# Block-selected attention and a gated network: a new recorded order of the five queues

## The chip, the cores and the metric

One core of a Trainium2 chip. The metric is the device time of one execution in microseconds (us). The kernel before took 310.41, 308.06 and 309.83 us in three runs, median 309.83.

In the profile PE is TensorE (PEld its weight loads), DVE is VectorE, ACT is ScalarE, POOL is GpSimd, SP is SyncE, which only issues transfers. L949 is line 949 of the kernel before.

## What is computed

Attention over 4 batches, 8 heads, 768 positions and 64 channels, in which each query sees only the 6 chunks of 32 keys with the highest upper bounds; then, on the 3072 tokens of 512 channels that come out, an RMS norm and a gated network of width 1536.

```python
k_min, k_max = k_chunks.min(axis=3), k_chunks.max(axis=3)
ub = sum(maximum(q * k_min, q * k_max), axis=-1)      # upper bound of each chunk
top_chunks = argsort(where(causal, ub, -1e9))[..., -6:]
scores = where(selected & (pos_q >= pos_k), scale * q @ k.T, -1e9)
attn_out = softmax(scores) @ v
xn = x / sqrt(mean(x * x) + 1e-6) * rms_g              # x: attn_out, heads side by side
g = xn @ w_gate
out = ((g * sigmoid(g)) * (xn @ w_val)) @ w_out
```

## The kernel before

The work is cut into twelve blocks of 256 tokens, (batch, third of the sequence), in the order of the list `ORDER`: (0,0), (1,0), (2,0), (3,0), (0,1), (1,1), (0,2), (2,1), (1,2), (3,1), (2,2), (3,2). "Block 0" below is (0,0). A block has an attention part for each of two groups of four heads, a norm, and a network part.

**Attention part.** SP (at the start ACT too) loads `kraw`, `qraw`, `vraw`. VectorE transposes them into `kT`, `qT` (`turn k`, `turn q`, L621) and takes the minimum and maximum of each chunk (`ext`, L636). `half k` and `half q` (L628, L629) convert to bf16 on ScalarE or GpSimd. TensorE forms the upper bounds (`upper`, L507 or L525), VectorE turns them round (`ubn`, L550), finds the sixth largest (`top`, L566), compares (`mk`, L572) and turns the mask back (`mt`, `swap`). TensorE forms the scores (L749) with the mask added by matmul (L760), ScalarE the exponential (L799), GpSimd zeroes the triangle (`tri`, L769), TensorE multiplies by the values (`values`, L825), VectorE divides (`rden` L840, `norm` L844). From the second third on, a copy of the queries (`qx`, L677) and four transfers (`qm`, L691) and a clamp (`relu`, L715) prepare the bounds.

**Norm.** ScalarE sums squares (L861), GpSimd takes the root (`rms`, L867, L869), `scale` multiplies each token by it (L893 on VectorE or L895 on ScalarE in the first four blocks, L879 on VectorE later), and a transpose on TensorE (`turn`, L905, then `xsT`) or by a transfer (`across`) gives `xsT`.

**Network part.** For each 256 columns of the hidden width (a "piece"; six pieces of a 256-token block, or pieces of 512 columns for one token half): a gate matmul group `wg` and a value group `wv` (L949, eight matmuls of 256 columns each), `tanh` of the gate on ScalarE (L956), `tg` on VectorE (L960), and then the product `hh` of `tg` and the value. In a piece listed in `DIRECT` VectorE forms the product straight from PSUM (L964); in the others ScalarE first copies the value out (`vcopy`, L968) and GpSimd forms the product (L971). `DIRECT` holds every second piece of blocks 4 to 11. Twelve hidden tiles go through `project` (L996), and `out` and `store` end the block.

**Order.** Every operation is entered into a plan with its reads, writes and buffers. Nothing is scheduled at run time and no order is searched when the kernel is built: `SEQUENCE` is a recorded permutation of the 1580 operations, `SLOTS` gives the buffer number of each tile, `CHOICE` the engine of each operation that has alternatives (`flex`), and `WARM` inserts groups of filler matmuls on TensorE (place in the sequence, count, PSUM buffer, 512 columns or 128). Each engine runs its operations strictly in the order in which `SEQUENCE` has them, and waits where an input or a buffer is not ready. There are 4 PSUM buffers `F` (bounds, gates, values, projections), 2 of `S` (scores), 2 of `kraw`, 3 each of `th`, `tg`, `vs`, 13 of `hh`.

**Weights.** Gate, value and output weights come in three pieces each (`wg0` to `wg2`, `wv0` to `wv2`, `wo0` to `wo2`), 512 KB each, issued by GpSimd. `GATES` lets them follow the operation `dk(0, 0, 0)`, and a chain keeps them in the order in which the plan lists them. The loads of block 2 are fenced on the landing of `wg1`, those of block 3 on `wo0` and `wo1` (`HELD`).

Of the kernel before, what the change touches and what calls it, by code (L numbers as in the profile page):

```python
# [10 lines left out]
ALU = mybir.AluOpType  # L11
ACT = mybir.ActivationFunctionType
# [121 lines left out]
    "ADDADA")  # L134
WARM = [
    (58, 86, 0, 0), (72, 4, 2, 1), (97, 10, 0, 1), (140, 6, 2, 1), (166, 2, 3, 1), (174, 5, 2, 1), (183, 1, 1,
    1), (267, 1, 3, 1), (339, 1, 0, 1)]


class Op:  # L140
# [964 lines left out]
```

## Time and profile before

| | us |
|---|---|
| median of three runs | 309.83 |
| profiled execution, its span | 305.9 |
| PE busy | 285.5 |
| DVE busy | 226.8 |
| ACT busy | 204.3 |
| POOL busy | 162.5 |
| exponentials, ACT L799, 104 | 86.2 |
| `tg`, DVE L960, 72 | 48.5 |
| products on GpSimd, L971, 48 | 55.8 |
| products on VectorE, L964, 24 | 16.2 |
| HBM read and written | 28.58 MB, 6.29 MB |

A row of the timeline has the start, the length, the engine, the line, the operation, output and input and the count. A row of the groups has the busy time of all of them, the mean of one in ns, and the idle time before them with what ended it. A row of the windows has, for each engine, its busy time and the instructions it touches, then the granted TensorE clock and the share and rate of the DMA engines. The rows themselves stand with the prediction.

### The profile page before, as it was taken

To read this page: it belongs to the slowest core of one execution; us is meant where nothing else is said; L and a number is where in the kernel's file an instruction comes from. 1 tells how busy PE (TensorE), PEld (TensorE's weight loads), DVE (VectorE), ACT (ScalarE), POOL (GpSimd) and SP (SyncE) were. 2 spreads that over 40 slices of the span, in tenths; PEclk is the share of its full clock that TensorE was granted. 3 is DMA by queue.
4 is the path that set the end of the run, shared out by engine and by line. 5 is a ranking of instruction groups with operands and counts; after the bars stand their busy time and mean duration, and the time that the engine had idled before them with its cause. 6 is when DMAs were issued, how large, how long until landed. Compare 5 with 4: busy or idle time off the path is not lost.

```text
span 305.9 us, 11386 instructions
## 1 busy us (share of the span) xinstructions
PE 285.5 (93%) x4672; PEld 217.5 (71%) x4672; DVE 226.8 (74%) x633; ACT 204.3 (67%) x353; POOL 162.5 (53%) x272
## 2 busy tenths in 40 slices
PE   7889697999999997899999996999999999999994
PEld 7567585666966865788766685678877876778763
DVE  4976979959999999679999995978545445155441
ACT  3698557457867985787987684488865776665501
POOL 4887869476964979464656443407442324214130
PEclk9999889799999999999999999899999999999999
DMA  6999999447465659456666666501103004012011
GB/s 209 208 199 198 230 181 191 86 115 162 94 163 134 153 122 173 108 130 142 158 157 132 152 153 130 133 2 27 46 2 106 2 3 105 3 71 70 2 69 69
DMA packets 86388, 35.08 MB, mean 115 GB/s; under 512 B 74816, under 2 KB 81728, under 8 KB 86336
## 3 DMA queue, kind: packets, MB, share of 16 engines
q1 hardware_dynamic: 80736, 29.12, 40.3%
q0 software_dynamic: 4752, 4.72, 9.6%
q8 instruction: 36, 0.59, 0.8%
q10 hardware_dynamic: 848, 0.53, 0.6%
q14 instruction: 16, 0.13, 0.1%
HBM read 28.58 MB, written 6.29 MB: 114 GB/s over the span
## 4 chain that ended last, share of the span: by engine, by line
PE 52%; DVE 18%; DMA 12%; SPq 6%; POOL 4%; issue 4%; ACT 2%; ACTq 0%; DVEq 0%; POOLq 0%
PE F L949 25%; PE F L996 14%; PE S L749 5%; PE F L825 5%; SPq L354 4%; DMA kraw<-in_k_dram 4%; DVE kx L636 3%; DMA QX<-qT 2%; DMA wg<-in_moe_w_gate_dram 2%; DMA qraw<-in_q_dram 2%; DVE kT L621 2%; PE S L760 2%; DVE tg L960 2%; DVE xs L879 2%; DVE m L566 2%
## 5 line engine op out<-in xcount | busy, mean ns | idle before, releaser
L799 ACT ACTIVATE pt<-S 128x1024 bf16<-128x1024 f32 (+3 forms) x104 | 86.2, 859 | 28.4 <-PE S L760 26.9
L971 POOL TENSOR_TENSOR hh<-tg,vs 128x512 bf16<-128x512 bf16 x48 | 55.8, 1168 | 41.1 <-DVE tg L960 21.4
L949 PE MATMUL F<-xsT,wg 128*128 128x256 bf16 (+1 forms) x608 | 73.4, 270 | 3.4 <-DMA wg<-in_moe_w_gate_dram 1.8
L949 PE MATMUL F<-xsT,wv 128*128 128x256 bf16 (+1 forms) x608 | 73.6, 270 | 2.5 <-DVE tg L960 2.4
L996 PE MATMUL F<-wo,hh 128*128 128x512 bf16 (+1 forms) x300 | 68.8, 373 | 1.8 <-POOL hh L971 0.6
L960 DVE SCALAR_TENSOR_TENSOR tg<-th,F 128x512 bf16<-128x512 bf16 x72 | 48.5, 678 | 27.8 <-ACT th L956 24.3
L949 PEld LDWEIGHTS <-wg 128*128 128x128 bf16 x608 | 56.2, 99 | 12.7 <-DMA wg<-in_moe_w_gate_dram 2.1
L949 PEld LDWEIGHTS <-wv 128*128 128x128 bf16 x608 | 56.3, 99 | 11.6 <-issue 2.8
L956 ACT ACTIVATE th<-F 128x512 bf16<-128x512 f32 x72 | 42.5, 599 | 24.5 <-PE F L949 23.2
L996 PEld LDWEIGHTS <-hh 128*128 128x128 bf16 x300 | 28.0, 98 | 29.0 <-issue 2.2
L769 POOL TENSOR_SCALAR_AFFINE_SELECT pt<-pt 128x512 bf16<-128x512 bf16 x48 | 31.3, 658 | 28.8 <-ACT pt L799 28.6
L825 PE MATMUL F<-VX,pt 128*128 128x65 bf16 x672 | 28.8, 195 | 7.2 <-DVE tg L960 3.0
L968 ACT ACTIVATE vs<-F 128x512 bf16<-128x512 f32 x48 | 28.6, 601 | 9.8 <-PE F L949 5.7
L825 PEld LDWEIGHTS <-pt 128*128 128x128 bf16 x672 | 26.7, 99 | 11.1 <-issue 6.7
L749 PE MATMUL S<-qb,kb 32*128 32x256 bf16 (+1 forms) x800 | 33.6, 258 | 0.1
L636 DVE TENSOR_REDUCE kx<-kT 128x16 f32<-128x512 f32 x48 | 30.7, 667 | 0.2
L964 DVE TENSOR_TENSOR hh<-tg,F 128x512 bf16<-128x512 bf16 x24 | 16.2, 677 | 12.6 <-PE F L949 12.1
L749 PEld LDWEIGHTS <-kb 32*128 32x128 bf16 x800 | 13.8, 93 | 10.4 <-issue 9.2
L760 PE MATMUL S<-mtd,chunkrow 32*128 32x128 bf16 (+2 forms) x384 | 20.6, 206 | 0.0
L844 DVE TENSOR_TENSOR xnat<-F,rden 128x256 bf16<-128x256 f32 x48 | 19.9, 419 | 1.0
L861 ACT ACTIVATE junk<-xnat 128x512 bf16<-128x512 bf16 x24 | 15.1, 631 | 8.0 <-DVE xnat L844 6.6
L760 PE MATMUL S<-mto,chunkrow 32*128 32x128 bf16 (+2 forms) x384 | 20.2, 205 | 0.1
(73 smaller groups left out, 346.7 us busy)
## 6 DMA issues: line engine op xcount, KB each, us to landing
vraw<-in_v_dram SPq DMA_DIRECT2D x24, 256.0 KB, 3.6
out_dram<-osb SPq DMA_DIRECT2D x23, 256.0 KB, 2.5
kraw<-in_k_dram SPq DMA_DIRECT2D x72, 64.0 KB, 3.0
qraw<-in_q_dram SPq DMA_DIRECT2D x72, 64.0 KB, 2.8
QX<-qT SPq DMA_DIRECT2D x32, 64.0 KB, 2.2
wg<-in_moe_w_gate_dram POOLq DMA_DIRECT2D x3, 512.0 KB, 7.4
wv<-in_moe_w_val_dram POOLq DMA_DIRECT2D x3, 512.0 KB, 8.0
wo<-in_moe_w_out_dram POOLq DMA_DIRECT2D x3, 512.0 KB, 9.6
```

The source lines that it names most:

```text
L636: plan.op(f"ext{n}{J}", "DVE", 0.585, 0.67, lambda n=n, op=op: VE.tensor_reduce(out=at(kx)[:, g, n], in_=at(kT).rearrange("p h (j c x) -> ...
L749: TE.matmul(s[a // 2][:, a % 2, c0:c0 + q1 - q0], kbt[r, t, ks], qbt[r, t, q0:q1], start=(t == 0), stop=(t == 1 and not mask), skip_group_ ...
L760: TE.matmul(o, chunkrow[r, BLK * kg + P * e:BLK * kg + P * (e + 1)], mv, start=False, stop=(d == 1), skip_group_check=True)
L769: GE.affine_select(out=d, in_=d, compare_op=ALU.is_ge, fill=0.0, base=0, pattern=[[0, 4], [1, P]], channel_multiplier=-1)
L799: lambda pt=pt, hs=hs, c0=c0, c1=c1, x=sc[hp]: SE.activation(out=at(pt)[:, hs, c0:c1], in_=at(x)[:, :, c0:c1], func=ACT.Exp, scale=SCALE), ...
L825: TE.matmul(o[:, a, :], p_[:, a, off:off + P], vt[:, e, a, :], start=(kb_ == 0 and a == 0), stop=(kb_ == nkb - 1 and a == 3), skip_group_c ...
L949: TE.matmul(at(p_)[:, n * W:(n + 1) * W], w[:, g, ht * P:(ht + 1) * P], at(xT)[:, g, x0:x0 + W], start=(g == 0), stop=(g == NP - 1), skip_ ...
L956: plan.op(f"tanh{U}.{hp}", "ACT", 0.48, 0.6, lambda th=th, gp=gp: SE.activation(out=at(th), in_=at(gp), func=ACT.Tanh, scale=0.5), pri - 0 ...
L960: VE.scalar_tensor_tensor(out=at(tg), in0=at(th), scalar=1.0, in1=at(gp), op0=ALU.add, op1=ALU.mult), pri - 30, reads=[th, gp], writes=[tg ...
L968: plan.op(f"vcopy{U}.{hp}", "ACT", 0.48, 0.6, lambda vs=vs, vp=vp: SE.activation(out=at(vs), in_=at(vp), func=ACT.Copy), pri + 0.1, reads= ...
L971: plan.op(f"hh{U}.{hp}", "POOL", 1.11, 1.16, lambda tg=tg, vs=vs, hh=hh: GE.tensor_tensor(out=at(hh), in0=at(tg), in1=at(vs), op=ALU.mult) ...
L996: TE.matmul(at(op)[:, cs], at(key)[:, o:o + P], wo[:, ht, cs], start=(ht == 0), stop=(ht == NHT - 1), skip_group_check=True)
```

## The change

`SEQUENCE`, `SLOTS`, `CHOICE` and `WARM` are replaced. The plan has 1604 operations, as all 72 products now have a value copy entered before them, of which 23 are void; otherwise its operations stay the same but for three points.

Each product `hh` now has two engines to choose from. Where `CHOICE` gives VectorE, it reads the value from PSUM and the `vcopy` before it is void (`N`): it isn't issued and takes no buffer. `DIRECT` goes. The chosen products on VectorE are 23 (24 before): 4 in block 0, 1 in block 2, 2 in block 3, 1, 2, 1, 3, 4, 1, 2, 2 in blocks 4 to 11.

```diff
-    DIRECT = {(i, hp) for i in range(len(ORDER)) for hp in range(KH) if i >= 4 and hp % 2}
...
-            if (i, h0 // 2) in DIRECT:
-                plan.op(f"hh{U}.{hp}", "DVE", 0.6, 0.69, lambda tg=tg, vp=vp, hh=hh: VE.tensor_tensor(
-                    out=at(hh), in0=at(tg), in1=at(vp), op=ALU.mult), pri - 20, reads=[tg, vp],
-                    writes=[hh], takes=[(hh, "hh")])
-                continue
...
+            spare = flex(f"vcopy{U}.{hp}", {
+                "ACT": (0.48, 0.6, lambda vs=vs, vp=vp: SE.activation(out=at(vs), in_=at(vp), func=ACT.Copy)),
+                "NONE": (0.0, 0.0, None)}, pri + 0.1, reads=[vp], writes=[vs], takes=[(vs, "vs")])
+            flex(f"hh{U}.{hp}", {
+                "POOL": (1.11, 1.16, lambda tg=tg, vs=vs, hh=hh: GE.tensor_tensor(
+                    out=at(hh), in0=at(tg), in1=at(vs), op=ALU.mult)),
+                "DVE": (0.6, 0.69, lambda tg=tg, vp=vp, hh=hh: VE.tensor_tensor(
+                    out=at(hh), in0=at(tg), in1=at(vp), op=ALU.mult))}, pri - 10, reads=[tg, vs],
+                writes=[hh], takes=[(hh, "hh")]).pair = spare
```

The weights lose their gates and their chain, and the load of `rmsg` its place behind those of the first queries:

```diff
-    GATES = {"0": "dk(0, 0, 0)", "1": "dk(0, 0, 0)", "2": "dk(0, 0, 0)", "o": "dk(0, 0, 0)"}
...
-    plan.ops[-1].after.append([o for o in plan.ops if o.dma and o.name.startswith("load q00")][-1])
...
-            named = {o.name: o for o in plan.ops}
-            for x, y in GATES.items():
-                for nm in ("wg", "wv") if x != "o" else ("wo",):
-                    named[nm + (x if x != "o" else "0")].deps.append(named[y])
-            chain = [o for o in plan.ops if o.dma and o.eng == "POOL"]
-            for x, y in zip(chain, chain[1:]):
-                y.after.append(x)
```

In `Plan.run`:

```diff
+        void = {x for x, e in engine.items() if e == "N"}
...
+            if x in void:
+                continue
...
-            for key in o.uses:
+            instead = o.pair.uses if o.pair is not None and o.pair.seq in void else []
+            assert (o.pair is None) or (o.pair.seq in void) == (o.eng == "DVE")
+            for key in o.uses + instead:
+                if self.taker[key].seq in void:
+                    continue
```

The fillers:

```diff
-WARM = [
-    (58, 86, 0, 0), (72, 4, 2, 1), (97, 10, 0, 1), (140, 6, 2, 1), (166, 2, 3, 1), (174, 5, 2, 1), (183, 1, 1,
-    1), (267, 1, 3, 1), (339, 1, 0, 1)]
+WARM = [
+    (51, 42, 0, 1), (77, 6, 2, 1), (96, 2, 2, 1), (115, 2, 0, 1), (129, 1, 0, 1), (161, 3, 1, 1), (173, 3, 2,
+    1), (185, 5, 0, 1)]
```

Engine by engine, with the counts of before in brackets: conversions of keys and queries on ScalarE 24 (17), on GpSimd 24 (31); copies `qx` on ScalarE 9 (4), GpSimd 7 (11), VectorE 0 (1); `scale` of blocks 0 to 3 on ScalarE 6 (2), VectorE 2 (6); products on GpSimd 49 (48), value copies 49 (48). The operations of TensorE other than the fillers are the same.

On GpSimd's queue the weight pieces now stand in the order `wg1`, `wg0`, `wv0`, `wv1`, `wg2`, `wo0`, `wv2`, `wo1`, `wo2` (before: `wg0`, `wv0`, `wg1`, `wv1`, `wg2`, `wv2`, `wo0`, `wo1`, `wo2`). `wg1` stands behind the second `dk` of block 0; `wg0` behind the first two triangles and a `dk` of block 1; `wv0` behind the first `rms`; `wg2` behind the second `rms` and the first triangles of block 1. On TensorE the first gate group stands behind the first two values of block 1 and the second transpose of block 0; before, it stood behind the first transpose. On VectorE both comparisons `mk` of block 2 stand ahead of the `tg` of hidden tile 6 of block 1; the product of that `tg` is the first of block 1 in GpSimd's queue, with its other products of block 1 behind it.

More of the change, by code (lines that the diff above doesn't have):

```diff
@@ L150, in __init__ @@
         self.mode = None
+        self.pair = None
         self.done = None
@@ L155 @@
 class Plan:
-    NAMES = {"P": "PE", "A": "ACT", "D": "DVE", "G": "POOL", "S": "SP"}
+    NAMES = {"P": "PE", "A": "ACT", "D": "DVE", "G": "POOL", "S": "SP", "N": "NONE"}
     def __init__(self):
@@ L213, in run @@
             assert all(d.seq in gone for d in o.deps + o.after) and x not in gone
+            gone.add(x)
             if x in engine:
                 o.eng = self.NAMES[engine[x]]
+            if x in void:
+                continue
             o.occ, o.lat, o.fn = o.alts[o.eng]
@@ L220, in run @@
                 held[place_] = key
-            for key in o.uses:
+            instead = o.pair.uses if o.pair is not None and o.pair.seq in void else []
[3 more added lines that the diff above has]
+                    continue
+                assert held[self.pool_of[key], self.slot[key]] == key
                 left[key] -= 1
@@ L224, in run @@
                     held[self.pool_of[key], self.slot[key]] = None
-            gone.add(x)
             order.append(o)
```

16 lines of the change are left out of this document (6 added, 10 removed), and 221 rows, old and new, of tables (SEQUENCE, SLOTS).

## The prediction

> **What bounds the kernel now.** I read the page's head and its busy slices first.
>
> ```profile
> span 305.9 us, 11386 instructions
> PE 285.5 (93%) x4672; PEld 217.5 (71%) x4672; DVE 226.8 (74%) x633; ACT 204.3 (67%) x353; POOL 162.5 (53%) x272
> ...
> PE   7889697999999997899999996999999999999994
> ...
> DVE  4976979959999999679999995978545445155441
> ```
>
> TensorE is busy 93% of the span, VectorE nearly always until slice 26 (about 200 us), and seldom after. So the second view cuts the span where the stages change: to the first matmul of the gated network (21.55), to the end of its second block (75), to the last attention score (202), to the tail.
>
> ```profile
> core 0: us, PE busy (x) PEld busy (x) DVE busy (x) ACT busy (x) POOL busy (x), PEclk, DMA share, GB/s
> 0.00:21.55 21.55, 17.61 (x350) 13.68 (x351) 15.47 (x52) 12.82 (x24) 15.46 (x57) 1.00 0.93 206
> 21.55:75.00 53.45, 48.26 (x706) 36.68 (x703) 45.47 (x110) 33.41 (x68) 37.09 (x58) 0.94 0.84 167
> 75.00:202.00 127.00, 119.65 (x2198) 90.28 (x2199) 115.56 (x365) 95.98 (x161) 77.66 (x116) 0.99 0.61 136
> 202.00:300.00 98.00, 97.92 (x1420) 75.57 (x1413) 49.86 (x108) 61.15 (x100) 32.34 (x42) 1.00 0.14 40
> 300.00:305.90 5.90, 2.03 (x16) 1.33 (x14) 0.42 (x1) 0.98 (x2) 0.00 (x0) 1.00 0.24 89
> ```
>
> The fourth stage, 98 us, is TensorE's alone (97.92 busy): no order of the others helps there, and the matmuls themselves are the same before and after. What can change is the 21.55 us before the first gate, the 5.2 idle us of the second stage (53.45 less 48.26) and its half-speed clock, and the 7.35 idle us of the third (127.00 less 119.65), where VectorE is busy 115.56 of 127 and sets the pace. The third view, the chain of waits, says what holds the second stage:
>
> ```profile
> 32.96 2.92 DVE xs L893
> ...
> 47.85 2.88 POOL hh L971 x3
> ...
> 51.18 0.63 POOL pt L769
> 51.82 0.56 POOL VX L731
> 52.38 0.59 POOL pt L769
> 52.97 0.68 DVE tg L960
> 53.69 1.86 PE F L949 x16
> ...
> 274.89 13.97 PE F L949 x128
> ```
>
> The last row is full speed: 128 matmuls in 13.97 us, 0.109 each, 0.87 for a group of eight. GpSimd work followed by a VectorE step stands on the chain, and the timeline shows why:
>
> ```profile
> 19.71 0.35 DVE L893 TENSOR_SCALAR xs<-xnat,ri_all 128x512 bf16<-128x512 bf16 x1 [1.75 <-POOL ri_all L869]
> 32.88 3.00 DVE L893 TENSOR_SCALAR xs<-xnat,ri_all 128x512 bf16<-128x512 bf16 x1
> 47.89 0.44 DVE L582 STREAM_TRANSPOSE mto<-mk 64x32 bf16<-64x32 bf16 x2
> 48.37 4.67 DVE L572 TENSOR_TENSOR mk<-ubn,m 128x64 bf16<-128x64 f32 x1
> ```
>
> The same scaling takes 0.35 us and 3.00 us; the small comparison at 48.37 takes 4.67 and ends where GpSimd's unbroken run (47.85 to 52.97 in the chain) ends. VectorE is locked out by a busy GpSimd, for 2.65 us at the one and over 4 at the other, and everything in its queue waits. The Trainium skill, SBUF — State Buffer, section "Who interferes with whom", says that such a VectorE instruction and GpSimd take a shared port in turn, for a whole instruction; the 4.67 us here span six GpSimd instructions, not one, so the trace has it worse.
>
> **Part by part: the start.** In the new order the first filler on TensorE is 42 matmuls of 512 columns that read `chunkrow`, instead of 86 of 128 columns that read only `ident`. Rows of the timeline, and two of the windows:
>
> ```profile
> 1.75 6.85 PE L1072 MATMUL F<-ident 128*128 128x128 bf16 x86 [1.75 <-POOL ident masks.py:199]
> 2.21 0.55 DVE L393 TENSOR_SCALAR chunkrow<-pat 128x768 bf16<-128x768 bf16 x1
> 5.06 1.30 DVE L621 STREAM_TRANSPOSE kT<-kraw 128x512 f32<-128x512 f32 x2 [2.31 <-DMA kraw<-in_k_dram]
> 9.44 0.29 PE L749 MATMUL S<-qb,kb 32*128 32x128 bf16 x8
> 10.44 0.64 ACT L799 ACTIVATE pt<-S 128x256 bf16<-128x256 f32 x2
> 11.45 2.33 PE L1072 MATMUL F<-chunkrow,ident 128*128 128x512 bf16 x10
> 12.54 0.99 POOL L354 DMA_DIRECT2D wg<-in_moe_w_gate_dram  x1
> 21.55 0.61 PE L949 MATMUL F<-xsT,wg 128*128 128x128 bf16 x8
> 4.00:5.00 1.00, 1.00 (x12) 1.00 (x11) 0.00 (x0) 0.18 (x1) 0.00 (x0) 1.00 0.76 234
> 7.00:8.00 1.00, 1.00 (x22) 1.00 (x20) 1.00 (x3) 0.50 (x1) 0.88 (x8) 1.00 0.86 260
> ```
>
> A warm wide filler costs about 0.22 us (2.33 for ten, the last one's drain taken off). The first 4 us of matmuls run at half rate (12 in flight per us at 4, 22 at 7). From about 3.0 (`chunkrow` done at 2.76, one small copy put ahead of it) nine go in 4 us, and 33 by 0.22 end near 14. The first scores follow there, not at 9.44, and the first exponentials near 14.5 instead of 10.44. VectorE starts about 1 us later than 5.06 (two loads of the next block stand between those it needs), then waits some 2.5 us for the upper bound, which stands behind filler and scores, and has three more 0.65 us steps (two reductions and a transpose) ahead of the first scaling: 19.71 becomes about 25. Behind that, ScalarE puts two exponentials and a conversion ahead of the first `xsT`, and GpSimd a norm ahead of the triangle that TensorE needs before its first gate. I get the first gate at about 31.5 instead of 21.55. By 31.5 the old order had done seven groups of eight gate matmuls, 7 by 0.87 = 6.1, and a few scores; the new one has done none, and nothing else instead: **7 us behind** (bounds 3, if the loads hide part, and 10, the whole shift).
>
> **The second stage** then has 7 us more of matmuls to do than the old from 31.5 on, so it reaches the same point 7 us later less what it no longer loses. The old order lost 8.4 in this stage: 5.2 idle, and 6% of 53.45 for a granted clock of 0.94, 3.2. Of these the lockouts go: the scalings of blocks 0 to 2 move to ScalarE (only the first of all and one of block 3 stay), and both comparisons of block 2 stand on VectorE ahead of the `tg` for which GpSimd's next run of products waits, so that GpSimd idles then. With the 4.67 goes its restart at half clock (first a row of the waits, then windows; the rows of groups and of a transfer below them are for the next terms):
>
> ```profile
> PE F L949 <- DVE tg L960: 2.4, 1, 2.4
> ...
> 36.00:38.00 2.00, 1.65 (x17) 1.41 (x17) 1.95 (x5) 1.23 (x4) 1.03 (x1) 0.61 1.23 205
> 38.00:40.00 2.00, 2.00 (x18) 1.75 (x17) 0.85 (x3) 1.44 (x4) 0.34 (x2) 0.53 1.24 209
> 54.00:56.00 2.00, 2.00 (x35) 1.69 (x37) 1.91 (x5) 0.00 (x0) 0.00 (x0) 0.50 0.48 92
> L895 ACT ACTIVATE xs<-xnat,ri_all 128x512 bf16<-128x512 bf16 x2 | 1.4, 722 | 0.7 <-POOL ri_all L869 0.6
> L964 DVE TENSOR_TENSOR hh<-tg,F 128x512 bf16<-128x512 bf16 x24 | 16.2, 677 | 12.6 <-PE F L949 12.1
> L677 DVE COPY QX<-qT 128x512 f32<-128x512 f32 x1 | 1.4, 1379 | 0.0
> wg<-in_moe_w_gate_dram POOLq DMA_DIRECT2D x3, 512.0 KB, 7.4
> ```
>
> I take 5.5 off, between 0 and 8: 4.1 for the comparison (2.4 idle, when the gate waited for the `tg` behind it, and 1.7 for 3.4 us at half clock), and for the scaling half of its 2.65, as TensorE had other work beside it. Four products of block 0 now run on VectorE at 0.68, 2.7 us, paid from the 7 us the lockouts took. The weights in free order work both ways. Gate piece 1 is issued first; the loads of the third block, fenced on its landing, start some 5 us earlier than before. But pieces 0 and 2 are queued on GpSimd behind triangles and norms: the first near 18.5 instead of 12.54, piece 2 near 31; with 7.4 us to land, both come just when TensorE gets to them. I count no gain and no loss, with up to 2 either way. Net to the 75 us point: 7 − 5.5 = **+1.5** (−2 to +8).
>
> **The third stage.** Before, 24 of the 72 products were on VectorE, all from block 4 on; now 23, six to seven of them before block 4. That leaves about four fewer here (2.7), and one copy of 1.38 goes to another engine: 4 us less on the engine that is busy 91%. ScalarE gets five more such copies and several conversions, about 6 us on 95.98 of 127, which it can hold if its queue does not wait. VectorE enters the stage about where it did: the 7 us of lockouts pay for its 5 us late start and the 2.7 of early products. TensorE can win at most its idle 7.35 and a little stretch; I take the 4.1 of VectorE and 0.4 for eight fewer instructions on GpSimd that could lock it out, **−4.5** (−9 to +8: the idle time with its stretch below, as much again above for an in-order queue that waits at the wrong place). The fourth stage and the tail keep their form, 0 (−1 to +2).
>
> Sum: 305.9 + 1.5 − 4.5 = 302.9 us of span. The span of before is 3.9 under its median of 309.83, and I add the same: **about 306.8**, 1% less.
>
> **The rivals.** *The late gates are never made up* (slower): TensorE enters its 98 us of unbroken work with whatever it is behind. If VectorE's queue is paced by `tanh` and scores rather than by its own work, the third stage returns nothing and the start's 7 stay: 309.8 + 6 = 316. It decides from about 4 us of lag at 75 us. For: TensorE is full late. Against: VectorE's 91%. *The third stage opens wide*: with no lockout VectorE runs ahead, and the 7.35 idle us and stretched steps go: −9 in place of −4.5, and the start's bound of 3 in place of 7: 306.8 − 4.5 − 4 = 298, or 300 with some of it kept. *ScalarE becomes the bound* between 75 and 202, its added work colliding with exponentials that scores wait for: +4 or so, 313. *Nothing net*: start and lockouts cancel and the moved products only trade engines: 310. *The clock*: the stretches of 1.5 to 2 us without matmuls that I expect between 18 and 31 us let the clock fall as it did at 36 and 54 (0.5 to 0.6), and the first gates run at half speed for 3.4 us, 1.7 more: 308.5 (306.8 and 1.7). The Trainium skill, TensorE: Matmul & The Clock Gate, section "What's actually happening", has the clock fall after an idle window of about 3.4 us; the 0.50 after 2.4 us idle shows that less can do. That the order is not followed is no rival: each queue of the built program stands as recorded.
>
> **How the numbers follow.** Forecast 0.30, wide opening 0.27, late gates 0.20, ScalarE 0.10, nothing net 0.07, clock 0.06. Between runs 1% (306.7 to 312.9) is about what can be told. The forecast's own spread is 303 to 310.5, half of it below 306.7: faster 0.15 + 0.27 = 0.42; same 0.15 + 0.07 + 0.06 = 0.28; slower 0.20 + 0.10 = 0.30. The range runs from 298 (a third of the wide opening left out) to 316 (half of the late gates left out); its own likeliest part is the forecast's 303 to 310.5.
>
> **What would show it.** First gate near 31 us (right about the start) or below 26 (wrong); first exponential near 14.5. No `mk` or `xs` on VectorE over 2 us before 60 us; a lockout of the same size there would make the second stage wrong. Second block's last projection near 76. Between 75 and 200, TensorE idle under 4 us means the third stage is right; over 10, with ScalarE or VectorE waiting for `th`, that the first rival or ScalarE won. Wrong altogether if weights hold TensorE for over 3 us.

## The result and the profile after

The changed kernel took 312.55 us (median of four runs, 310.87 to 314.07); the kernel before, beside it, 309.02. The ratio is 1.0114 with a 95% interval of 1.0065 to 1.0163: slower by 1%. The same kernel run again later, six times beside 23 runs of the kernel before (308.50), took 314.34, ratio 1.0247 (1.0175 to 1.0320). Medians here are over all runs, while a ratio and its interval compare only each kernel's fast runs (the same program also has slower ones), so a ratio is not the quotient of the two medians beside it; by those the second comparison gives 1.0189. The two intervals do not meet, so an interval tells how well one comparison is known, not how the next will come out. Over all ten runs the median is 313.77, 5.0 above the mean of the two 309.02 and 308.50. The forecast was 306.8, faster by 1%; the direction was wrong.

The page's head, its busy slices, and the same cut by stages as before (to the first gate, to 75, to 202, to the tail):

```profile
span 309.2 us, 11258 instructions
PE 288.2 (93%) x4620; PEld 212.9 (69%) x4620; DVE 217.8 (70%) x628; ACT 214.3 (69%) x373; POOL 155.2 (50%) x258
...
PE   5979999769999999799999899999999999999994
...
PEclk9987999959999999999999999999999999999998
```

```profile
0.00:32.42 32.42, 25.88 (x361) 13.80 (x362) 21.04 (x72) 17.98 (x35) 17.00 (x59) 0.89 1.04 194
32.42:75.00 42.58, 37.85 (x571) 29.48 (x568) 30.47 (x76) 28.57 (x57) 25.07 (x42) 0.92 0.93 169
75.00:202.00 127.00, 121.37 (x2176) 91.21 (x2175) 111.18 (x343) 103.14 (x177) 76.20 (x113) 1.00 0.61 133
202.00:305.00 103.00, 102.80 (x1521) 78.39 (x1519) 55.08 (x139) 63.97 (x104) 36.97 (x47) 1.00 0.15 43
```

VectorE is 9 us lighter (226.8 to 217.8), of it 4.4 in the third stage (115.56 to 111.18), where 4 were forecast, and TensorE's share of the span is the same 93%. From 202 us on TensorE has 103.1 us of work left (102.80 and 0.28) instead of 99.95 (97.92 and 2.03): it is about 3 us behind. The clock row has a new 5 in its ninth slice, 62 to 70 us. The timeline of the start:

```profile
3.47 10.97 PE L1076 MATMUL F<-chunkrow,ident 128*128 128x512 bf16 x42 [3.47 <-DVE chunkrow L407]
14.37 0.29 PE L763 MATMUL S<-qb,kb 32*128 32x128 bf16 x8
14.70 0.38 ACT L813 ACTIVATE pt<-S 128x256 bf16<-128x256 f32 x1 [1.85 <-PE S L763]
32.42 1.82 PE L963 MATMUL F<-xsT,wg 128*128 128x128 bf16 x23
```

Filler to 14.4, first exponential at 14.70 (14.5 forecast), first gate at 32.42 (31.5): the start went as worked out. (Line numbers are 14 higher than before from the attention part to the gate and value matmuls; the product on GpSimd is now L981, the projection L1008, the filler L1076.) What the forecast did not have stands in the second stage. First the chain of waits, then GpSimd's rows of the timeline, then TensorE's and three windows with the clock:

```profile
46.47 8.28 DMA kraw<-in_k_dram
...
59.21 4.37 DMA vraw<-in_v_dram
...
63.70 0.62 POOL VX L745
64.32 0.04 issue
64.36 0.60 PE F L839 x8
```

```profile
56.97 0.64 POOL L783 TENSOR_SCALAR_AFFINE_SELECT pt<-pt 128x512 bf16<-128x512 bf16 x1
61.99 0.22 POOL L656 TENSOR_TENSOR kx<-kx 128x16 f32<-128x16 f32 x1 [4.38 <-DVE kx L650]
63.70 0.61 POOL L745 CAST VX<-vraw 128x512 bf16<-128x512 f32 x1 [1.49 <-DMA vraw<-in_v_dram]
```

```profile
64.36 0.60 PE L839 MATMUL F<-VX,pt 128*128 128x65 bf16 x8 [4.15 <-POOL VX L745]
...
61.65:64.40 2.75, 0.04 (x2) 0.04 (x2) 0.74 (x2) 0.79 (x2) 0.92 (x3) 0.50 1.14 201
64.40:68.48 4.08, 4.08 (x25) 2.49 (x25) 3.75 (x9) 1.52 (x3) 3.27 (x8) 0.50 0.88 189
68.48:72.00 3.52, 3.52 (x28) 1.81 (x27) 2.19 (x8) 2.62 (x6) 1.80 (x2) 1.00 1.12 221
```

TensorE stands 4.15 us before the values of block (2,0), and runs at half speed for 4.1 us more. GpSimd's cast of v, which it waits for, has two waits in a row: 4.38 us behind block (3,0)'s difference of key extents (L656), which stands ahead of it in GpSimd's queue, and 1.49 us for v itself. SP's waits say why both came late:

```profile
SPq L368 <- DMA wo<-in_moe_w_out_dram: 19.1, 1, 19.1
```

The new order puts the two loads of v of block (2,0) behind the first load of block (3,0), and that one is fenced on the landing of `wo0`. SP stood from 22.9 to 42.0 us. v was issued at 58.1 us, behind 22 other loads; in the order before it went out at 40.4, second after the fence.

A measure for the rest: the start of the last projection matmul of block 2. Up to there both orders have run the same network matmuls, the new one 16 score and 16 mask matmuls more, about 0.5 us. It stands at 97.8 us before and at 104.1 after:

```profile
L996 PE MATMUL F<-wo,hh x24: 377/379/379, 87.7 to 97.8; 128*128 128x512 bf16 x24
```

```profile
L1008 PE MATMUL F<-wo,hh x24: 379/379/390, 94.4 to 104.1; 128*128 128x512 bf16 x24
```

So nearly 6 us are lost by there (6.3, less 0.5 of work done in advance), and what follows returns about 3 in this trace (208.1 us from there to the end before, 205.1 after). "Block 2's mark" below is this start. Traces with the same order up to it agree there to 0.2 us (104.1 and 103.9 for the changed kernel, 100.2 and 100.4 with the earlier fence below), so single traces can be compared at it; from it to the end they differ by some 4 us.

The prediction's own sign for this stage, the second block's last projection near 76 us, came at 77.6, close to the forecast. But TensorE had then done 256 gate and value matmuls, where the order of before had done 280 at 75.3: the same event, with less work behind it.

### The profile page after: what moved, and what is told of

The parts are those of the page before. It is cut to its first block, busy times and chain, and to the rows that moved or that the text cites. A ratio compares the mean times of both kernels' runs of the same rounds, so it can differ in the third digit from the quotient of the medians.

```text
span 309.2 us, 11258 instructions
## 1 busy us (share of the span) xinstructions
PE 288.2 (93%) x4620; PEld 212.9 (69%) x4620; DVE 217.8 (70%) x628; ACT 214.3 (69%) x373; POOL 155.2 (50%) x258
## 4 chain that ended last, share of the span: by engine, by line
PE 62%; DMA 14%; DVE 8%; SPq 5%; POOL 4%; ACT 3%; issue 2%; ACTq 0%; DVEq 0%; POOLq 0%
PE F L963 26%; PE F L1008 16%; PE S L763 5%; PE F L839 5%; SPq L368 5%; PE F L1076 4%; DMA xsT<-xs 4%; DMA vraw<-in_v_dram 3%; DMA wv<-in_moe_w_val_dram 3%; DMA kraw<-in_k_dram 3%; PE S L774 2%; POOL hh L981 2%; PE F L521 2%; DVE kx L650 1%; DVE tg L974 1%
## 5 line engine op out<-in xcount | busy, mean ns | idle before, releaser
L813 ACT ACTIVATE pt<-S 128x1024 bf16<-128x1024 f32 (+3 forms) x104 | 85.1, 859 | 18.2 <-PE S L774 14.2
L981 POOL TENSOR_TENSOR hh<-tg,vs 128x512 bf16<-128x512 bf16 x49 | 56.4, 1163 | 53.3 <-DVE tg L974 28.7
L963 PE MATMUL F<-xsT,wv 128*128 128x256 bf16 (+1 forms) x608 | 72.1, 267 | 2.9 <-DMA xsT<-xs 2.5
L1008 PE MATMUL F<-wo,hh 128*128 128x512 bf16 (+1 forms) x300 | 68.6, 374 | 0.4 <-POOL hh L981 0.4
L963 PEld LDWEIGHTS <-wv 128*128 128x128 bf16 x608 | 55.5, 98 | 13.3 <-issue 2.6
L1008 PEld LDWEIGHTS <-hh 128*128 128x128 bf16 x300 | 28.2, 99 | 27.9 <-POOL hh L981 1.1
L978 ACT ACTIVATE vs<-F 128x512 bf16<-128x512 f32 x49 | 29.3, 601 | 17.9 <-PE F L963 13.3
L839 PEld LDWEIGHTS <-pt 128*128 128x128 bf16 x672 | 25.5, 99 | 8.3 <-issue 4.3
L763 PEld LDWEIGHTS <-kb 32*128 32x128 bf16 x800 | 14.5, 93 | 16.2 <-issue 14.6
L1023 ACT ACTIVATE osb<-F 128x512 f32<-128x512 f32 (+1 forms) x19 | 10.9, 577 | 16.6 <-PE F L1008 16.4
L1076 PE MATMUL F<-chunkrow,ident 128*128 128x512 bf16 x64 | 18.0, 432 | 3.5 <-DVE chunkrow L407 3.5
L635 DVE STREAM_TRANSPOSE kT<-kraw 128x512 f32<-128x512 f32 x24 | 16.4, 693 | 6.9 <-DMA kraw<-in_k_dram 6.5
L774 PE MATMUL S<-mto,chunkrow 32*128 32x128 bf16 (+2 forms) x384 | 20.7, 203 | 0.3 <-ACT mto L600 0.2
```

The lines of the kernel that those rows point to most:

```text
L763: TE.matmul(s[a // 2][:, a % 2, c0:c0 + q1 - q0], kbt[r, t, ks], qbt[r, t, q0:q1], start=(t == 0), stop=(t == 1 and not mask), skip_group_ ...
L774: TE.matmul(o, chunkrow[r, BLK * kg + P * e:BLK * kg + P * (e + 1)], mv, start=False, stop=(d == 1), skip_group_check=True)
L813: lambda pt=pt, hs=hs, c0=c0, c1=c1, x=sc[hp]: SE.activation(out=at(pt)[:, hs, c0:c1], in_=at(x)[:, :, c0:c1], func=ACT.Exp, scale=SCALE), ...
L839: TE.matmul(o[:, a, :], p_[:, a, off:off + P], vt[:, e, a, :], start=(kb_ == 0 and a == 0), stop=(kb_ == nkb - 1 and a == 3), skip_group_c ...
L963: TE.matmul(at(p_)[:, n * W:(n + 1) * W], w[:, g, ht * P:(ht + 1) * P], at(xT)[:, g, x0:x0 + W], start=(g == 0), stop=(g == NP - 1), skip_ ...
L981: "POOL": (1.11, 1.16, lambda tg=tg, vs=vs, hh=hh: GE.tensor_tensor(out=at(hh), in0=at(tg), in1=at(vs), op=ALU.mult)),
```

## The experiments

Theory 1 at first: v behind the fence is the loss. Theory 2: the late start is the loss. Numbers in `SEQUENCE` are operations: 221 and 222 the two loads of v of block (2,0), 249 its cast, 296 the first load of block (3,0), 319 that block's difference of key extents. In the expectations "piece 4" to "piece 6" are blocks 4 to 6, and "VX" is what the cast of v writes.

### The hole at 59 us

**v ahead of the fence:**

```diff
+SEQUENCE = [x for x in SEQUENCE if x not in (221, 222)]
+SEQUENCE[SEQUENCE.index(296):SEQUENCE.index(296)] = [221, 222]
```

> The changed kernel with the two loads of v of block (2,0) put in SP's order right ahead of the first load of block (3,0), which is fenced on wo0; nothing else. Theory 1 (the 4.98 us hole at 59 us is v arriving late, and it is the whole of what the changed kernel lost in its second stage): the hole closes, TensorE is 4 to 5 us earlier from 64 us on and nothing later gives it back, so about 308 us, 4.5 below the changed kernel's 312.5 and within 1% of the kernel before. Theory 2 (the late start is the loss; the hole only holds what would wait anyway, for masks or for the product of the feed-forward part): the hole closes in name, another wait of 3 us or more stands within the next 15 us, and the time stays within 1 us of 312.5. Theory 3 (the two loads ahead of wg and wv delay the first weights): the first gate, at 32.4 us in the changed kernel, moves back by over 1 us.

311.69 us, ratio 1.0069 (1.0028 to 1.0110). Block 2's mark comes at 100.4, 3.7 earlier than in the changed kernel, near theory 1's 4 to 5; but the time fell by 1 to 3 us, not 4.5. And 1.6 us of the hole stay, although v is there:

```profile
57.54 0.63 POOL L783 TENSOR_SCALAR_AFFINE_SELECT pt<-pt 128x512 bf16<-128x512 bf16 x1
60.91 0.22 POOL L656 TENSOR_TENSOR kx<-kx 128x16 f32<-128x16 f32 x1 [2.74 <-DVE kx L650]
61.08 0.61 POOL L745 CAST VX<-vraw 128x512 bf16<-128x512 f32 x1
```

The cast follows the key extents without a wait for v: of the two waits the one underneath is left.

**v behind the fence, but first behind it** (the insertion one place later):

> The changed kernel with the two loads of v of block (2,0) right behind the first load of block (3,0), so still behind the fence on wo0, which opened at 42.1 us, but ahead of the 21 other loads that stood between. If the depth of the queue behind the fence is what made v late: v is issued near 42.6 us and lands near 48, ten us before its values, and the time is that of the run with v ahead of the fence, within 1 us. If the fence itself is what matters (all loads of that time crowd together when it opens, and each lands 5 us or more after its issue): half of the gain or less, 310 to 312 us. If theory 2 holds: no change, 312.5.

316.46 us, ratio 1.0269 (1.0219 to 1.0318): above the changed kernel's 312.55 and 314.34, though the interval overlaps that of its second comparison. So nothing is gained; of the three only theory 2's "no change" is near, and for another reason. v is in time, but the keys of block (3,0) are later still, and GpSimd stands for them:

```profile
64.73 0.22 POOL L656 TENSOR_TENSOR kx<-kx 128x16 f32<-128x16 f32 x1 [7.16 <-DVE kx L650]
```

So the depth of the queue is not it either: whatever stands first behind the fence makes the other late, and GpSimd's queue needs both.

**v ahead of the fence, and its cast ahead of the key extents:**

```diff
+SEQUENCE = [x for x in SEQUENCE if x not in (221, 222, 249)]; i = SEQUENCE.index(296)
+SEQUENCE[i:i] = [221, 222]; SEQUENCE.insert(SEQUENCE.index(319), 249)
```

> The changed kernel with v of block (2,0) ahead of the fence as in the first run, and on GpSimd its copy into VX put right ahead of block (3,0)'s difference of key extents, behind which it stood. The traces so far: with v there by 26 us the copy still began at 61.08, behind that difference, which waited 2.7 us for extents that VectorE makes of keys which SP loads only when the fence opens. Theory 1b (the hole at 59 us has two waits, v's arrival and, under it, GpSimd's stand for block (3,0)'s keys): with both out of the way the copy begins at 58 us, the hole is under 0.6 us (4.98 in the changed kernel, 1.8 with v alone), and TensorE is 4.5 to 5 us ahead of the changed kernel at 65 us; at the end 2 to 5 us stay, 308 to 310.5. Theory 2b (block (3,0)'s selection itself is late, and the next values wait for it anyway): the hole closes and opens again at block (3,0)'s scores near 75 us; 311 to 312.5, as with v alone.

310.45 us, ratio 1.0066 (1.0032 to 1.0100). The cast begins at 57.07 and no longer holds the values. Two short waits of 0.7 us together stay there, and one of 1.80 us for `tg` follows at 62.85. Block 2's mark: 101.4. Theory 1b names the waits rightly; what opens next takes back part.

**The fence itself earlier**, all orders as they are:

```diff
-    HELD = {2: (("wg", 1), ("wg", 1)), 3: (("wo", 0), ("wo", 1))}
+    HELD = {2: (("wg", 1), ("wg", 1)), 3: (("wv", 0), ("wo", 1))}
```

> The changed kernel with only the fence of block (3,0)'s loads moved from the landing of wo0 (SP stood from 22.9 to 42.1 us) to the landing of wv0, some 9 us earlier; all orders as they are. In every trace so far SP is never idle for more than 0.6 us a time between 60 and 180 us, and the transposing transfers of pieces 4 and 6 start 2.5 to 6 us after their rows are scaled. Theory 3 (SP's queue is what holds the second and third stage, and the fence is why it is behind): the hole at 59 us closes, the waits for transposed rows at 126 and 173 us shrink together below 2 us from 3.6, and the time falls by 4 to 7 us, to 305.5 to 308.5. Theory 1b: only the hole closes, -2 to -5 us. Rival: the early loads share the DMA engines with wv1, wg2 and wo0, TensorE waits for weights for over 2 us between 35 and 60 us, and the time stays at 311 to 314.

310.70 us, ratio 1.0055 (1.0007 to 1.0104). All that TensorE waits for between 30 and 75 us is now:

```profile
PE F L963 <- DMA wv<-in_moe_w_val_dram: 1.4, 1, 1.4
PE S L763 <- ACT pt L813: 0.7, 1, 0.7
```

```profile
L1008 PE MATMUL F<-wo,hh x24: 379/379/390, 90.6 to 100.2; 128*128 128x512 bf16 x24
```

The hole is gone, block 2's mark is at 100.2, 3.9 earlier. Theory 1b's -2 to -5 holds; theory 3's further gain did not come: the waits for transposed rows later on stayed at 4.3 us. The premise of this expectation, that SP is never idle there for over 0.6 us, was too strong: in the changed kernel's trace it waits 2.6 us once between 75 and 180.

### The late start

**The changed kernel with 30 instead of 42 fillers**, alone and with v ahead of the fence:

```diff
-    (51, 42, 0, 1), (77, 6, 2, 1), (96, 2, 2, 1), (115, 2, 0, 1), (129, 1, 0, 1), (161, 3, 1, 1), (173, 3, 2,
+    (51, 30, 0, 1), (77, 6, 2, 1), (96, 2, 2, 1), (115, 2, 0, 1), (129, 1, 0, 1), (161, 3, 1, 1), (173, 3, 2,
```

> The changed kernel with 30 instead of 42 wide instructions in the filler ahead of the first scores, everything else as it is. The filler would end at about 11.4 us instead of 14.4, and the inputs of the first scores were there at 11.9. Theory 1 (the start is only a part, and v's loads hang on the fence, not on the start): first scores near 12, first gate 1.5 to 2.5 us earlier, but the hole at 59 us opens by as much, since v still comes at 63.6: 0 to -1 us, 311.5 to 312.5. Theory 2 (the late start is the loss): -2 to -3 us, 309.5 to 310.5. A third way: the fence's weight wo0 is issued earlier with the earlier start too, and the hole moves along; then as by theory 2.

> Both edits together: v of block (2,0) ahead of the fence and the first filler 30 long. Theory 1: the sum of both, now that v doesn't hold values any more: -5 to -7 us of 312.5, so 305.5 to 307.5, and faster than the kernel before by 0.5 to 1%. Theory 2: what the shorter filler alone gives, 309.5 to 310.5. If VectorE, which has 7 us of selection work ahead of the first exp, sets the first gate and not the filler: as v early alone, near 308.

Alone 311.33 us, 1.0028 (0.9981 to 1.0076), block 2's mark 102.4; with v early 310.41 us, 1.0041 (1.0000 to 1.0081), mark 100.7. The start is worth 1.7 us at the mark and does not add up with v: with both, GpSimd stands 4.42 us for the key extents, as the keys do not come earlier with the start.

**The kernel before with the late start:**

```diff
-    (58, 86, 0, 0), (72, 4, 2, 1), (97, 10, 0, 1), (140, 6, 2, 1), (166, 2, 3, 1), (174, 5, 2, 1), (183, 1, 1,
+    (58, 42, 0, 1), (72, 4, 2, 1), (97, 10, 0, 1), (140, 6, 2, 1), (166, 2, 3, 1), (174, 5, 2, 1), (183, 1, 1,
```

> The kernel before with the changed kernel's first filler (42 wide instructions on the row of chunk numbers instead of 86 narrow ones), nothing else: the filler then ends near 14.4 us instead of 8.6, and the first scores, whose inputs are there before 9, come 5.5 us later. Theory 1 (the start's delay is mostly absorbed: the chain of the first blocks waits for VectorE and for weights anyway): 0 to +2 us of 309.0. Theory 2 (what the start loses stays lost): +4 to +6 us. In both the loads and weights hang on the first blocks' work and move with it.

312.96 us, ratio 1.0149 (1.0076 to 1.0222). First gate at 27.29, 5.7 late; block 2's mark at 101.2, 3.4 late. Nearer to theory 2: more than half of what the start loses stays lost.

```profile
L996 PE MATMUL F<-wo,hh x22: 377/379/379, 91.2 to 101.2; 128*128 128x512 bf16 x22
```

### VectorE's long stays

**The kernel before without them**, both, and the mask alone:

```diff
+SEQUENCE.remove(266)
+SEQUENCE.insert(SEQUENCE.index(246) + 1, 266)
...
-        engine = dict(zip((o.seq for o in self.ops if len(o.alts) > 1), CHOICE))
+        engine = dict(zip((o.seq for o in self.ops if len(o.alts) > 1), CHOICE)); engine[204] = engine[209] = "A"
```

> The kernel before with its two long stays of VectorE in the second stage taken away: the scaling of block (1,0) is given to ScalarE (VectorE's took 3.00 us at 32.88), and the second half's mask of block (2,0) (4.67 us at 48.37) is put right behind the first half's on VectorE, where GpSimd had not yet begun the stretch beside which it lay. The prediction's price for both was 5.5 us at most, the half of it on TensorE's path likely. If the stays are on TensorE's path: -2 to -5 us of the 309.0 of the kernel before. If they lie beside work that TensorE has anyway (the trace of before has no hole of TensorE over 1 us between 33 and 60 us but those of the clock): within 1 us. If the work that GpSimd does there only blocks VectorE's next instruction instead: another instruction of VectorE of over 2 us stands within 6 us of the same place, and the time is unchanged.

> The kernel before with only the mask of block (2,0)'s second half moved right behind the first half's (VectorE stayed 4.67 us in it at 48.37, and TensorE's wait of 2.44 us and the halved clock of 53.5 to 56.9 us follow), the scaling of block (1,0) left on VectorE. If the mask is the larger part of the 1.1% which both edits gave: ratio 0.990 to 0.994. If it is the scaling (3.00 us at 32.88, with TensorE's wait of 1.78 us and the halved clock from 36.4 us behind it): 0.997 to 1.001.

Both: 304.33 us beside 310.30, ratio 0.9887 (0.9825 to 0.9950), the fastest kernel of this study, and faster than both kernels. The mask alone: 306.11 beside 308.50, 0.9889 (0.9787 to 0.9991); that interval is too wide to divide the gain, and the mark below is the better witness that the mask is the larger part. The stay is shorter, not gone (4.67 us for one comparison before, 2.94 for both now):

```profile
47.06 2.94 DVE L572 TENSOR_TENSOR mk<-ubn,m 128x64 bf16<-128x64 f32 x2
```

```profile
L996 PE MATMUL F<-wo,hh x22: 376/379/379, 86.0 to 96.0; 128*128 128x512 bf16 x22
```

Block 2's mark moves by 1.8 (96.0) with both edits and by 1.2 (96.6) with the mask. The rest of the 3.5 us (1.13% of 310) lies later, where traces of one order differ by 4 us, and is not attributed.

### The third stage

**The changed kernel again:**

> The changed kernel as it is, once more. Its four runs so far (312.55, ratio 1.0114) stand against some 12 of each variant, and its one trace loses 12.8 us of TensorE in the third stage (from 40 to 130 us of its own work) where the traces of seven variants with the same third stage lose 14.3 to 20.8. If that trace is a lucky draw of the third stage, a second one loses 14 us or more there, its wait at 126 us is 2.3 to 4 us instead of 2.06, and the median of many runs stands at 312 to 315 (ratio 1.010 to 1.018); the hole at 59 us is there again, 3 to 6 us. If the edits that closed the hole made the third stage worse themselves, the second trace shows 12 to 13.5 again.

314.34 us, ratio 1.0247. The hole is there again (4.2 us), block 2's mark is at 103.9, and 209.5 us follow instead of 205.1. The wait at 126 us is 3.2 us now. So the first trace was a lucky draw of what follows block 2.

**Six products back on VectorE:**

```diff
+BACK = [1259, 1271, 1283, 1327, 1359, 1371]
+for x in BACK: SEQUENCE.remove(x); SEQUENCE.insert(max(map(SEQUENCE.index, (x - 1, x - 2))) + 1, x)
...
-        engine = dict(zip((o.seq for o in self.ops if len(o.alts) > 1), CHOICE))
+        engine = dict(zip((o.seq for o in self.ops if len(o.alts) > 1), CHOICE)) | {x: "D" for x in BACK} | {x - 1: "N" for x in BACK}
```

> The changed kernel with six products of the third stage (three of piece 4, one of piece 5, two of piece 6), which the change gave to GpSimd, back on VectorE, each right behind its product with the gate, their copies on ScalarE left out; the same function is computed. The prediction took 4.5 us out of the third stage for VectorE's lighter load. If VectorE's load is what bounds that stage: +2 to +4 us, 314.5 to 316.5. If SP's queue bounds it (theory 3) and VectorE has room: within 1 us of 312.5, perhaps faster, since a product on VectorE takes 0.68 us instead of 0.6 on ScalarE and 1.15 on GpSimd and so comes sooner.

313.85 us, ratio 1.0192 (1.0137 to 1.0247), between the changed kernel's two ratios: no cost that can be told from none. From block 2's mark to the end it takes 209.6 us, as the second trace of the changed kernel does (209.5; the first 205.1). That the stage is paced by VectorE's load finds no support, but two comparisons of the changed kernel lie 1.3% apart, so a cost of 2 us or so is not excluded.

**Transposing transfers put forward in SP's order**, first those of block 4 alone (with v early and the short filler), then with the fence earlier and three query transfers as well, then that with the short filler:

```diff
+SEQUENCE = [x for x in SEQUENCE if x not in (221, 222, 447, 449)]; i = SEQUENCE.index(296)
+SEQUENCE[i:i] = [221, 222]; i = SEQUENCE.index(663); SEQUENCE[i:i] = [447, 449]
```

```diff
+T = [663, 447, 449, 664, 666]; i = SEQUENCE.index(663); SEQUENCE = [x for x in SEQUENCE if x not in T + [626]]
+SEQUENCE[i:i] = T; SEQUENCE.insert(SEQUENCE.index(843) + 1, 626)
```

> The changed kernel with v of block (2,0) ahead of the fence, the first filler 30 long, and in SP's order the two transposing transfers of piece 4 put ahead of four loads and one query store that stood before or between them; TensorE waited 2.06 us at 126.6 for the second of them, which SP issued at 126.5 although its rows were scaled by 121.7. If that wait is a queue's place and nothing else: 1.5 to 2 us below the run without this third edit. If the transfer's own time or the four loads behind it (queries of blocks (2,1) and (1,2)) take its place: within 0.7 us of that run, and a wait for queries shows in its stead.

> The changed kernel with the fence on wv0 (the hole at 59 us closed, ratio 1.0055 alone) and, in SP's order of the third stage, the transposing transfers of piece 4 and the query transfers qm0, qm1 and qm3 of block (2,1) ahead of eight loads of block (1,2), which are not needed for some 10 us, and the second transposing transfer of piece 6 ahead of five loads and stores. Theory 3 (third stage held by the place of such transfers in SP's order): the wait at 126 us (2.65 us with the fence alone) falls under 1 us, the one at 170 us (2.02) under 1.2 us, nothing over 2 us opens in their place, and the time falls by 2.5 to 4 us, to 307.0 to 308.5, so no slower than the kernel before. Rival (SP has no idle time there, so what is put back comes late in turn, as when only piece 4's transfers were moved): a wait for block (1,2)'s keys or queries, near 146 us, takes their place; within 1 us of 310.7.

> The same with the first filler 30 wide instructions long instead of 42. By the kernel before with the late start (+3.3 us in the trace at 60 us of TensorE's work, ratio 1.0149) and the changed one with the shorter filler alone (2 us at 20 us of TensorE's work): 1.5 to 2.5 us below the run without it, 305 to 307. If the first weights, which the earlier start meets sooner, hold it: the first wait for wv or wg grows by as much, and the time stays.

Here 447 and 449 are the transposing transfers of block 4, 626 the second of block 6, 663, 664, 666 and 843 query transfers (`qm`). The first: 312.97 us, 1.0149 (1.0078 to 1.0220), slower than without that edit. The wait at 126 us went. GpSimd's clamp of queries (L729) then waited longer (5.5 us without the edit), with a wait of 2.8 us of TensorE behind it; the clamp reads the query transfers that had been passed, so the transfer named is probably a neighbour of the one meant:

```profile
POOL qraw L729 <- DMA kraw<-in_k_dram: 7.0, 1, 7.0
```

That trace also has a wait of 3.54 us for an exponential at 32 us, far ahead of the edit, so its time says less than its rows.

The second: 309.61 us, 1.0114 (1.0045 to 1.0182); without the edit it was 310.70 and 1.0055. From block 2's mark to the end it takes 209.0 us, without the edit 207.8: nothing gained. The waits for transposed rows fell from 4.3 to 1.2 us, and the rival's wait came in their place: VectorE stood for the loads that had been passed, `tg` behind them in its queue, and TensorE for `tg`:

```profile
DVE kT L635 <- DMA kraw<-in_k_dram: 3.4, 1, 3.4
```

```profile
143.21 1.26 PE L839 MATMUL F<-VX,pt 128*128 128x65 bf16 x20 [3.26 <-DVE tg L974]
```

The third: 306.99 us beside 308.50, ratio 1.0005 (0.9959 to 1.0051): level with the kernel before, some 7 us under the changed one. There the same load held VectorE for 0.9 us only, and block 2's mark is at 97.5, 2.9 earlier than with the long filler (100.4): once the fence is open, the start is worth more than the 1.7 us it gave alone.

**SP's queue made shorter**, no order changed (stores of blocks 1 to 5 issued by ScalarE, v loads of blocks 4 to 11 by GpSimd), in the changed kernel with the earlier fence and in the kernel before without the stays; and, without that relief, an earlier fence (on `wv1`) in the latter:

```diff
-            dma(f"load v{b}{m}{e}", "SP", v[b, :, t0:t0 + P, :].rearrange("a p d -> p a d"),
+            dma(f"load v{b}{m}{e}", "SP" if i < 4 else "POOL", v[b, :, t0:t0 + P, :].rearrange("a p d -> p a d"),
...
-                o = plan.op(f"store{tag}", "SP", 0.46, 0.46, lambda ob=ob, r0=r0, cs=cs: SY.dma_start(
+                o = plan.op(f"store{tag}", "ACT" if 0 < i < 6 else "SP", 0.46, 0.46, lambda ob=ob, r0=r0, cs=cs, i=i: (SE if 0 < i < 6 else SY).dma_start(
```

> The kernel before without the two long stays of VectorE (as in the run with 304.3 us) and with the fence of block (3,0)'s loads on the landing of wv1 instead of wo0. SP stood from 29.8 to 40.0 us there and was idle for 7.8 us more between 60 and 80. Theory 3: SP gets 5 to 8 us ahead, the waits of that kernel for transposed rows and keys go, 301 to 303.5. If the loads were in time already (the trace without the stays shows no wait of TensorE for a transfer of SP's between 40 and 180 us over 1.3 us): within 1 us of 304.3. Rival as above: weights late, 305 to 308.

> The changed kernel with the fence on wv0 (1.0055 alone), and with SP's queue relieved without a change of order: the ten stores of blocks 1 to 5 are issued by ScalarE and the v loads of blocks 4 to 11 by GpSimd, at the same places of the sequence. Up to 126 us that is some 14 of the issues ahead of piece 4's transposing transfers, at 0.45 us or more each. Theory 3 (SP's queue has no slack in the third stage and every hole there is a transfer that came late through it): the transposing transfers of pieces 4 and 6 start within 1.5 us of their rows (3.2 to 6.2 us with the fence alone), TensorE's waits for transposed rows fall under 1.5 us in all (4.3), nothing of VectorE's queue waits for a load in their place, and the time falls by 2 to 4 us, to 306.5 to 308.5. Rival (the queues are in step, and what the new issues cost ScalarE and GpSimd, 5 to 10 us each, comes back as later copies and products): within 1 us of 310.5, with TensorE waiting for ScalarE's or GpSimd's work by as much.

> The same relief of SP's queue in the kernel before without the two long stays of VectorE (304.3 us, ratio 0.9887). In the kernel before the largest hole of the third stage, 3.02 us at 186.9, was put down to VectorE's product with the gate; VectorE had waited 3.1 us for the transfers of the queries, which SP issues. Theory 3: that wait goes, and the time falls by 1 to 3 us more, 301.5 to 303.5. Rival as for the other: within 1 us of 304.3, or slower by what ScalarE and GpSimd lose.

306.52 us, 0.9944 (0.9900 to 0.9988): no gain over 304.33. The relieved ones: 315.60 us, 1.0222 (1.0144 to 1.0301), and 307.97, 1.0037 (0.9997 to 1.0076), both slower than without the relief. GpSimd is busy 14 us longer than in the changed kernel:

```profile
PE 286.9 (91%) x4594; PEld 213.4 (68%) x4620; DVE 218.2 (70%) x628; ACT 214.5 (68%) x373; POOL 169.0 (54%) x274
```

Most of the loss in the first lies ahead of block 2's mark: that is at 104.5, 4.3 later than with the fence alone, and 209.3 us follow instead of 207.8. In the second it is 97.8 instead of 96.0, then 208.6 instead of 205.7. TensorE's waits for transposed rows fell from 4.3 to 3.3 us only, where under 1.5 was expected. Theory 3, that the number of issues in SP's queue holds the third stage, finds no support in this form. That what the issues cost GpSimd and ScalarE outweighed what SP gained is the likely reason, and is not shown by itself.

## Why the prediction was wrong

**The start was right in its times and too dear in its price.** First exponential, first scaling and first gate came within 1 us of the forecast (14.70, 25.4 and 32.42 against 14.5, 25 and 31.5). For its price, 7 us between 3 and 10, the kernel before with the same filler loses 3.4 us at block 2's mark: near the lower end.

**The lockouts were right in kind, and too dear as well.** The mask and the scaling do stay long beside a busy GpSimd and lie on TensorE's path; without them the kernel before is 1.1% faster. At block 2's mark that is 1.8 us, not 5.5. In the changed kernel they are gone, as the prediction said; the two comparisons of block 2:

```profile
48.65 0.21 DVE L586 TENSOR_TENSOR mk<-ubn,m 128x64 bf16<-128x64 f32 x1
49.63 0.21 DVE L586 TENSOR_TENSOR mk<-ubn,m 128x64 bf16<-128x64 f32 x1
```

**The two errors cancel, by luck.** 3.4 less 1.8 is 1.6; the changed kernel with the earlier fence has 1.9 (100.2 less 97.8, less 0.5 of work in advance), and the prediction's net was +1.5.

**The first failed step** is the sentence on the weights and the loads: "I count no gain and no loss, with up to 2 either way." It priced when the weights land, and "wrong altogether if weights hold TensorE for over 3 us" looked for the fault there too. The weights came as it said (`wg0` was issued at 18.53 us, `wg2` at 32.04; 18.5 and 31 forecast) and held TensorE for 0.3 us. What it left out is the fence that hangs on them. SP reached it 6.9 us earlier than before (22.9 against 29.8) and the landing of `wo0` opened it 2.0 later (42.0 against 40.0), so SP stood 19.1 us instead of 10.2. The loads of v, second behind the fence before, now stood 22 loads behind it. In GpSimd's queue the keys' extents of block (3,0) and the cast of v came late one behind the other. That costs 3.9 us at block 2's mark (104.1 against 100.2), shown by the fence alone.

**The second failed step** is the -4.5 of the third stage. From block 2's mark to the end, five traces of the old order (before, late start, without one or both stays, earlier fence) took 208.1 us in the mean (205.7 to 210.7) and eight of the new one (the changed kernel twice, and the edits of the second stage and the start) 207.8 (205.1 to 212.3), or 207.1 without the slowest of them, the run with v first behind the fence. As 0.5 us of this is work done in advance, the gain is between nothing and 0.5, with traces of one order 4 us and more apart. The prediction read VectorE's 115.56 busy of 127 as the pace. VectorE did become 4.4 us lighter there, yet TensorE's idle time in that stage fell only from 7.35 to 5.63 us (127.00 less 121.37). Its own trace had a row against that, which it did not ask for. The largest hole of that stage, 3.02 us ahead of values at 189.88, is put down to VectorE's `tg`; but VectorE came late to it, as it had stood idle for 3.09 us just before, waiting for the query transfers that SP issues:

```profile
189.88 1.17 PE L825 MATMUL F<-VX,pt 128*128 128x65 bf16 x20 [3.02 <-DVE tg L960]
```

```profile
186.96 1.24 DVE L715 TENSOR_SCALAR qraw<-QX 128x512 f32<-128x512 f32 x1 [3.09 <-DMA QX<-qT]
```

A lighter VectorE meets the same late transfers. In the changed kernel TensorE waits for one directly: the second transfer of transposed rows of block 4 was issued at 126.54, 4.9 us after its rows were scaled:

```profile
126.54 1.19 SPq L899 DMA_TRANSPOSE xsT<-xs  x1
```

```profile
129.11 1.03 PE L963 MATMUL F<-xsT,wv 128*128 128x256 bf16 x8 [1.90 <-DMA xsT<-xs]
```

Shown: the forecast gain did not come although VectorE got lighter; a transfer put forward made another late in two of three runs; fewer issues on SP, paid by GpSimd and ScalarE, did not help. Six products more or less on VectorE made no difference that can be told from the spread. Not shown: which one queue sets the pace of the third stage, if one does. The runs agree best with several in-order queues in step, where one transfer, cast or product that comes late is passed on; that was not taken apart further.

**The sum.** Forecast, with the term of the weights and loads apart: +1.5, 0 and -4.5. Measured: +1.9, +3.9 and between 0 and -0.5, together +5.3 to +5.8, against the 5.0 of the medians. Of the rivals, the late gates that are never made up named the right outcome for part of the reason: the third stage returns almost nothing. Its 316 stood on a lag of 7 us from the start alone. The clock rival's fall came too, but from 20.7 to 27.5 us, ahead of the gates it was to slow.

## What to carry to other kernels

When a load moves in an in-order queue, list what it now stands behind, fences first, and then follow each consumer on its own queue: the hole here had two waits in GpSimd's queue, v and the key extents, both behind SP's fence, and moving v alone left the other. An engine that is busy 91% of a stage is not yet its pace: ask of the largest hole what the engine named was itself waiting for. And where traces of one order differ by 4 us, a term of 4.5 us needs several traces on each side before it is believed.

## What was not expected of the hardware

Holes cost more than their length. In the changed kernel TensorE idles 1.93 us at the start and then runs at half clock for 6.83 us; the 4.15 us at 60 are followed in the same way (the two windows at 0.50 further up).

```profile
18.76:20.69 1.93, 0.00 (x0) 0.09 (x1) 1.84 (x10) 1.54 (x2) 1.90 (x5) 1.00 0.39 64
20.69:27.52 6.83, 6.83 (x154) 4.66 (x154) 5.08 (x29) 4.04 (x9) 3.88 (x7) 0.50 1.14 225
```

The Trainium skill, TensorE: Matmul & The Clock Gate, section "What's actually happening", has a free-running window of 3413 ns and a fall of the clock after an idle one. The lengths agree, 6.83 being two of them; the threshold does not: 1.93 us without a matmul was enough here.
